# Unpacking the first MLP's wide weights through two tiles instead of one

## The chip, the cores and the metric

One NeuronCore of a Trainium2 chip runs the whole program. The metric is device time in microseconds (us) from the start to the end of one execution; smaller is better.

## The reference

```python
def reference(...):                               # float64 inputs, float32 result
    attn = g * mem_out + (1 - g) * softmax(causal(q @ k.T / 8)) @ v    # 4 x 8 heads, 576 x 64
    x = attn.transpose(0, 2, 1, 3).reshape(2304, 512)
    h = x @ w_in                                  # moe_w_in 512 x 2048, first MLP
    g = where(h > 0, h, exp(min(h, 0)) - 1)       # ELU
    x = g @ w_out                                 # moe_w_out 2048 x 512
    h = x @ w2_in                                 # second MLP, same sizes
    return maximum(0.01 * h, h) @ w2_out          # leaky ReLU
```

`mem_out` is a linear-attention read of a stored memory. The weights arrive as 64-bit floats. [...]

## The kernel before

**Blocks.** The 2048 hidden units of an MLP are 16 blocks of 128, called block 0 to 15 here (`f` in the code, `NF` = 16). A block's input and output weights go together into one weight place, a tile `w0`, `w1`, ... of 128 x 2 x 2 x 512: the rounded part ("hi") and the remainder ("lo") of 2 x 512 weights, so that three matmuls (hi x hi, lo x hi, hi x lo) give nearly full precision. The pool `wpa` has 7 places for blocks 0 to 6 (`NFA` = 7), the pool `wpb` 9 places for blocks 7 to 15. The second MLP's blocks use the same places later.

**Stages.** While attention still runs, TensorE already computes blocks 0 to 6 of the first MLP for "narrow" parts of 288 tokens, eight in all. Their partial products are copied out of PSUM to tiles `st` by ScalarE and stored to DRAM (`ys0` to `ys7`). After attention the last narrow parts end, and blocks 7 to 15 follow in five "wide" passes over 512 tokens (the last has 256). The second MLP then runs in wide passes with all 16 blocks.

**One block of work.** `h_mm` gives the hidden units (12 matmuls into one of four PSUM banks, two tagged `pm` and two `tp`). `elu` does a Relu and an Exp on ScalarE and a combining step on VectorE, which is the last reader of the bank; `g_split` casts the result to `gh` on VectorE and subtracts to get `gl` on GpSimd. The output product takes 12 matmuls more from `gh` and `gl` (`o_mm`).

**Unpacking** (`load_w`). For each block two transfers of 512 KB bring raw words into `wraw` (two buffers). Then: a ScalarE copy of the high words (L127) into a tile `wm`, three VectorE steps on 1024 int32 per partition (L128, L129, L132), a ScalarE cast to the hi part (L241), and two GpSimd subtractions to the lo part (L138). `wm` has one buffer in this stage (`nwm` = 1), so the next block's L127 waits for this block's second L138.

**Order.** A scheduler fixes, when the program is built, the order of instructions on every engine from priorities and its own estimates; each engine then executes its list in that order and waits on semaphores. The two `merge`d lists are the remaining narrow work (`side`) and the unpacking of blocks 7 to 12 (`NPRE` = 6); blocks 13 to 15 are unpacked within the first wide pass.

Of the kernel before, what the change touches and what calls it, by code (L numbers as in the profile page):

```python
# [9 lines left out]
F32R = mybir.dt.float32r  # L10
I32 = mybir.dt.int32
AF = mybir.ActivationFunctionType
ALU = mybir.AluOpType
AX = mybir.AxisListType

P = 128
# [3 lines left out]
def _f(ap):  # L20
    return ap.bitcast(F32)
# [3 lines left out]
def kernel(  # L25
# [14 lines left out]
    nc = tc.nc  # L40
    B, H, S, D = q.shape
    NT, DM = out.shape
# [3 lines left out]
    NF = DFF // P  # L46
    NFA = 7
    NPRE = 6
# [8 lines left out]
    E_GH, E_WH, E_VH, E_MS, E_V32, E_XH, E_RS, E_Y = "V", "A", "V", "P", "P", "A", "P", "A"  # L57
# [16 lines left out]
    wpa = ctx.enter_context(tc.tile_pool(name="wpa", bufs=1, side="left"))  # L74
# [18 lines left out]
    def load_w(key, pool, src_i, src_o, f, slot):  # L93

        w = pool.tile([P, 2, 2, DM], F32R, tag=f"w{slot}", name=f"w{slot}")
        wi_tiles[key, f] = w[:, :, 0].rearrange("p t (c n) -> p t c n", c=NKC)  # L100
        wo_tiles[key, f] = w[:, :, 1]
        raw = pools["wst"].tile([P, 2, DM, 2], I32, tag="wraw", bufs=2, name="wraw")
        nc.sync.dma_start(
            raw[:, 0].rearrange("p (c n) t -> p c (n t)", c=NKC),
            src_i[:, f * 2 * P:(f + 1) * 2 * P].rearrange("(c p) n -> p c n", p=P),
        )
        nc.sync.dma_start(raw[:, 1].rearrange("p n t -> p (n t)"), src_o[f * P:(f + 1) * P, :])
        if pools["decode_bank"]:
            for a in range(2):
                lw, hw = raw[:, a, :, 0], raw[:, a, :, 1]  # L110
                t = bank(pools["decode_bank"])
                m = t.bitcast(I32)
                nc.scalar.activation(out=t, in_=_f(hw), func=AF.Copy, scale=2.0 ** -112)
                nc.vector.tensor_scalar(out=m, in0=m, scalar1=3, scalar2=None, op0=ALU.logical_shift_left)
                nc.vector.scalar_tensor_tensor(
                    out=m, in0=lw, scalar=29, in1=m, op0=ALU.logical_shift_right, op1=ALU.bitwise_or
                )
                nc.vector.scalar_tensor_tensor(
                    out=m, in0=hw, scalar=-(1 << 31), in1=m, op0=ALU.bitwise_and, op1=ALU.bitwise_or
                )  # L120
                copy(E_WH, w[:, 0, a], t)
                nc.vector.tensor_tensor(out=w[:, 1, a], in0=t, in1=_f(w)[:, 0, a], op=ALU.subtract)
            return
        rw = raw.rearrange("p a n t -> p (a n) t")
        lw, hw = rw[:, :, 0], rw[:, :, 1]
        m = pools["wst"].tile([P, 2 * DM], I32, tag="wm", bufs=pools["nwm"], name="wm")
        nc.scalar.activation(out=_f(m), in_=_f(hw), func=AF.Copy, scale=2.0 ** -112)  # L127
        nc.vector.tensor_scalar(out=m, in0=m, scalar1=3, scalar2=None, op0=ALU.logical_shift_left)  # L128
        nc.vector.scalar_tensor_tensor(  # L129
            out=m, in0=lw, scalar=29, in1=m, op0=ALU.logical_shift_right, op1=ALU.bitwise_or  # L130
        )
        nc.vector.scalar_tensor_tensor(  # L132
            out=m, in0=hw, scalar=-(1 << 31), in1=m, op0=ALU.bitwise_and, op1=ALU.bitwise_or
        )
        t = _f(m).rearrange("p (a n) -> p a n", a=2)
        copy(E_WH, w[:, 0], t)
        for a in range(2):
            nc.gpsimd.tensor_tensor(out=w[:, 1, a], in0=t[:, a], in1=_f(w)[:, 0, a], op=ALU.subtract)  # L138
# [10 lines left out]
    def halves(n):  # L149
# [18 lines left out]
        out=mask[:, 448:576], in_=mask[:, 448:576], pattern=[[-1, 128]], compare_op=ALU.is_ge,  # L168
# [3 lines left out]
    pools = {"wst": wst_a.__enter__(), "nwm": 2, "decode_bank": "po"}  # L172
# [33 lines left out]
    def bank(tag):  # L206
        return psum.tile([P, 512], F32, tag=tag, bufs=BANKS[tag], name=tag)
# [30 lines left out]

    def copy(eng, dst, src):
        if eng == "A":  # L240
            nc.scalar.copy(dst, src)  # L241
        else:
            (nc.vector if eng == "V" else nc.gpsimd).tensor_copy(dst, src)  # L243

    def split(hi, lo, src, full=False):
        if full:
# [354 lines left out]
    def mtile(tag, bufs, dt=F32, shape=None):  # L601
        shape = shape or (NW,)
        pool = pools.get(("own", tag), pools["mlp"])
        return pool.tile([P] + list(shape), dt, tag=tag, bufs=bufs, name=tag)
# [12 lines left out]
    def h_mm(ph, wi, xh, xl):  # L617
        n_mm = 0
        for kc in range(NKC):
            for wj, xx in ((0, xh), (1, xh), (0, xl)):  # L620
                nc.tensor.matmul(ph, wi[:, wj, kc, :], xx[:, kc, :], start=n_mm == 0, stop=n_mm == 11)  # L621
                n_mm += 1

    def g_split(g, w):
        gh = mtile("gh", NG, F32R)[:, 0:w]
        gl = mtile("gl", NG, F32R)[:, 0:w]
        copy("A" if attending else E_GH, gh, g)
        nc.gpsimd.tensor_tensor(out=gl, in0=g, in1=_f(gh), op=ALU.subtract)  # L628
        return gh, gl

    def elu(ph, w):
        e = mtile("e", EB)[:, 0:w]
        nc.scalar.activation(out=e, in_=ph, func=AF.Relu, scale=-1.0)
        nc.scalar.activation(out=e, in_=e, func=AF.Exp, scale=-1.0)
        nc.vector.scalar_tensor_tensor(out=e, in0=e, scalar=-1.0, in1=ph, op0=ALU.add, op1=ALU.max)  # L635
        return g_split(e, w)

    def leaky(ph, w):
        t = mtile("e", EB)[:, 0:w]
# [4 lines left out]
    def o_mm(py, fs, key, ec, gs, first, last, opens=True, closes=True):  # L644
        for f in fs:
            wo = wo_tiles[key, f]
            gh, gl = gs[f]
            for n_mm, (wj, gg) in enumerate(((0, gh), (1, gh), (0, gl))):
                nc.tensor.matmul(  # L649
                    py, wo[:, wj, ec * P:(ec + 1) * P], gg,  # L650
                    start=opens and f == first and n_mm == 0, stop=closes and f == last and n_mm == 2,
                )

    attending = True
# [3 lines left out]
    def h_bank():  # L658
        nonlocal n_ph
        n_ph += 1  # L660
        return bank("tp" if tail and n_ph % 2 else "pm")
# [132 lines left out]
    attending = False  # L794
    edge = ctx.enter_context(tc.tile_pool(name="edge2", bufs=1, side="right"))
    edge.tile([P, 120], F32, name="edge2")
    wpb = ctx.enter_context(tc.tile_pool(name="wpb", bufs=1, side="right"))
# [3 lines left out]
    pools["xs"] = ctx.enter_context(tc.tile_pool(name="xs", bufs=1, side="right"))  # L801


    wun = [(1, lambda f=f: load_w(0, wpb, w1i, w1o, f, f - NFA)) for f in range(NFA, NF)]
    tail = True
    while ("cast", 1) not in pools:
# [8 lines left out]
    wun = wun[NPRE:]  # L815
# [32 lines left out]
    def load2(t0, n):  # L848
        xs = wide_x()
        for x, scr in zip(xs, xp_scr):  # L850
            recut(_f(x), scr, t0, n)
        return [x[:, :, 0:n] for x in xs]
# [6 lines left out]
    for gi, (t0, w) in enumerate(wide):  # L859
        gs = {}  # L860
        pys = {}

        def emit_out(f):
            for ec in range(NKC):
                if f == NFA:
                    pys[ec] = bank(("sc", "sc", "sc", "po")[ec])[:, 0:w]
                o_mm(pys[ec], [f], 0, ec, gs, NFA, NF - 1)
            del gs[f]

        ys = []  # L870

        def fetch_y():
            ne = NKC * TN // w
            for e in range(NKC // ne):
                yt = mtile("yx"[e], 1, F32, (ne, w))
                for pi, (_, _, pw, tok) in enumerate(parts):
                    lo, hi = max(tok, t0), min(tok + pw, t0 + w)
                    if lo < hi:
                        nc.sync.dma_start(
                            yt[:, :, lo - t0:hi - t0], y_scr[pi][:, ne * e:ne * e + ne, lo - tok:hi - tok]  # L880
                        )
                ys.extend(yt[:, i] for i in range(ne))

        for f in range(NFA, NF):
            if wun:
                wun.pop(0)[1]()
            if f == NFA + 3:
                fetch_y()
            ph = h_bank()[:, 0:w]
            h_mm(ph, wi_tiles[0, f], *cur)  # L890
            gs[f] = elu(ph, w)
            if f > NFA + 1:
                emit_out(f - 2)
            if gi >= 1 and f - NFA in (W2A, W2B) and len(w2) > NF - NFA:
                w2.pop(0)()
        emit_out(NF - 2)
        if gi + 1 < len(wide):
            cur = load2(*wide[gi + 1])
        emit_out(NF - 1)
        for ec in range(NKC):  # L900
            x1 = ys[ec]
            nc.vector.tensor_tensor(out=x1, in0=pys[ec], in1=x1, op=ALU.add)
            nc.sync.dma_start(x1_scr[gi][:, ec], x1)
# [81 lines left out]
```

## Time and profile before

| | us |
|---|---|
| median of 3 runs | 1069.39 (1069.12 to 1070.02) |
| the profiled execution | 1069.05 |
| span of its instructions | 1067.2 |
| TensorE busy | 1040.3 (97% of the span) |
| VectorE, ScalarE, GpSimd busy | 591.8, 485.2, 531.6 |
| granted TensorE clock | 0.996 of full speed |

The span is what the profile shows; the 1.85 us beside it lie before the first and after the last instruction. Attention ends at about 390 us, the last narrow part at about 452 us, the first wide pass lies from 441 to about 513 us.

### The profile page before, as it was taken

What the parts mean: (1) busy time and instruction counts of PE and PEld (TensorE: products, weight loads), DVE (VectorE), ACT (ScalarE), POOL (GpSimd) and SP (SyncE); (2) the same over time, 40 slices, a digit from 0 to 9 for tenths busy, and PEclk for the clock granted to TensorE, in tenths of its full rate; (3) what the DMA queues carried; (4) which work ended last, traced back from release to release, by engine and by line L of the source; (5) the groups of instructions that cost most, each with busy time, mean ns of one, the idle gap of its engine ahead of it and who ended that gap; (6) DMA issues with size and microseconds to landing.
All of it is one profiled execution on the core that took longest, in us unless ns stands there. A gap on an engine that the chain in (4) does not pass through costs nothing.

```text
span 1067.2 us, 17324 instructions
## 1 busy us (share of the span) xinstructions
PE 1040.3 (97%) x5904; PEld 909.9 (85%) x5904; DVE 591.8 (55%) x1380; ACT 485.2 (45%) x1171; POOL 531.6 (50%) x674
## 2 busy tenths in 40 slices
PE   7998899999999999999999999999999999999998
PEld 4786799989998999977888889888888888888897
DVE  6889987888888746566773324654322221232232
ACT  5999887787878735444442225332211211111111
POOL 7675775677668634464643225855422422322222
PEclk9999999999999999999999999999999999999999
DMA  7754553564456249465672304430200100000010
GB/s 183 195 150 112 160 142 96 139 166 142 115 128 164 90 113 337 147 223 168 227 232 85 119 1 138 158 119 1 80 1 1 60 20 1 8 33 1 1 40 20
DMA packets 150120, 115.05 MB, mean 108 GB/s; under 512 B 80016, under 2 KB 141456, under 8 KB 150032
## 3 DMA queue, kind: packets, MB, share of 16 engines
q1 hardware_dynamic: 149888, 113.68, 36.2%
q8 instruction: 47, 0.77, 0.3%
q14 instruction: 41, 0.34, 0.1%
q10 hardware_dynamic: 144, 0.26, 0.1%
HBM read 78.52 MB, written 31.85 MB: 103 GB/s over the span
## 4 chain that ended last, share of the span: by engine, by line
PE 80%; DVE 7%; DMA 4%; ACT 3%; issue 2%; POOL 2%; SPq 1%; DVEq 0%; POOLq 0%; ACTq 0%
PE pm L621 18%; PE sc L919 14%; PE tp L621 14%; PE sc L649 7%; PE pm L649 5%; PE po L919 4%; PE tp L457 4%; PE po L524 4%; PE pm L524 2%; PE po L649 2%; PE sc L426 2%; PE sc L428 1%; PE sc L429 1%; POOL w L138 1%; DMA wraw<-in_moe_w_in_dram 1%
## 5 line engine op out<-in xcount | busy, mean ns | idle before, releaser
L628 POOL TENSOR_TENSOR gl<-e,gh 128x512 fp32r<-128x512 f32 (+2 forms) x181 | 200.4, 1111 | 371.9 <-DVE gh L243 267.8
L621 PE MATMUL tp<-xw,w 128*128 128x512 f32 (+1 forms) x504 | 144.6, 367 | 1.7 <-DVE e L635 1.7
L621 PE MATMUL pm<-xw,w 128*128 128x512 f32 (+1 forms) x496 | 142.7, 369 | 1.2 <-ACT w L241 1.2
L919 PE MATMUL sc<-w,gh 128*128 128x512 f32 x448 | 135.9, 390 | 0.0
L451 POOL TENSOR_SCALAR pt<-pt,rs,omg 128x128 f32<-128x128 f32 (+4 forms) x160 | 104.1, 660 | 21.2 <-DVE rs L446 17.2
L621 PEld LDWEIGHTS tp<-xw,w 128*128 128x128 f32 x504 | 91.8, 188 | 18.3 <-DVE e L635 2.2
L621 PEld LDWEIGHTS pm<-xw,w 128*128 128x128 f32 x496 | 90.5, 188 | 17.7 <-ACT w L241 1.6
L436 ACT ACTIVATE pt<-pt,mx 128x128 f32<-128x128 f32 (+4 forms) x160 | 93.3, 585 | 23.2 <-DVE mx L431 21.6
L649 PE MATMUL sc<-gh,w 128*128 128x512 f32 (+2 forms) x438 | 103.2, 340 | 0.2 <-DVE gh L243 0.2
L919 PEld LDWEIGHTS sc<-w,gh 128*128 128x128 f32 x448 | 83.2, 188 | 16.5
L621 PE MATMUL tp<-xv,w 128*128 128x512 f32 (+1 forms) x252 | 92.6, 367 | 0.0
L621 PE MATMUL pm<-xv,w 128*128 128x512 f32 (+1 forms) x248 | 91.4, 369 | 0.0
L640 ACT ACTIVATE e<-pm 128x512 f32<-128x512 f32 (+1 forms) x40 | 22.2, 555 | 144.7 <-PE pm L621 141.7
L138 POOL TENSOR_TENSOR w<-wm,w 128x512 fp32r<-128x512 f32 x50 | 65.8, 1337 | 43.4 <-ACT w L241 39.4
L457 PE MATMUL tp<-ident,pt 128*128 128x128 f32 x480 | 82.0, 276 | 3.0 <-DVE al L250 1.5
L641 DVE TENSOR_TENSOR e<-tp,e 128x512 f32<-128x512 f32 (+1 forms) x40 | 25.5, 637 | 106.8 <-ACT e L640 106.8
L919 PE MATMUL sc<-w,gl 128*128 128x512 f32 x224 | 84.3, 389 | 0.0
L649 PEld LDWEIGHTS sc<-gh,w 128*128 128x128 f32 x438 | 74.6, 188 | 9.1 <-DVE gh L243 0.6
L641 DVE TENSOR_TENSOR e<-pm,e 128x512 f32<-128x512 f32 (+1 forms) x40 | 25.5, 637 | 102.1 <-ACT e L640 102.1
L621 PE MATMUL pm<-xh,w 128*128 128x288 f32 x368 | 79.6, 302 | 1.7 <-ACT xh L610 1.6
L243 DVE CAST gh<-e 128x512 fp32r<-128x512 f32 (+2 forms) x146 | 71.0, 490 | 13.5 <-PE po L919 3.0
L640 ACT ACTIVATE e<-tp 128x512 f32<-128x512 f32 (+1 forms) x40 | 22.2, 554 | 117.4 <-PE tp L621 117.4
(162 smaller groups left out, 2447.5 us busy)
## 6 DMA issues: line engine op xcount, KB each, us to landing
wraw<-in_moe_w_in_dram SPq DMA_DIRECT2D x32, 512.0 KB, 3.9
wraw<-in_moe_w_out_dram SPq DMA_DIRECT2D x32, 512.0 KB, 4.8
xh<-xh SPq DMA_DIRECT2D x8, 576.0 KB, 3.3
xl<-xl SPq DMA_DIRECT2D x8, 576.0 KB, 4.0
ys<-st SPq DMA_DIRECT2D x32, 144.0 KB, 2.8
x<-x1s SPq DMA_DIRECT2D x9, 512.0 KB, 3.8
vn<-in_v_dram SPq DMA_DIRECT2D x64, 64.0 KB, 2.4
out_dram<-st SPq DMA_DIRECT2D x32, 128.0 KB, 1.7
```

The source lines that it names most:

```text
L138: nc.gpsimd.tensor_tensor(out=w[:, 1, a], in0=t[:, a], in1=_f(w)[:, 0, a], op=ALU.subtract)
L243: (nc.vector if eng == "V" else nc.gpsimd).tensor_copy(dst, src)
L436: nc.scalar.activation(out=pt[0:m, 0:nk], in_=pt[0:m, 0:nk], func=AF.Exp, scale=-1.0, bias=mx[0:m, last:last + 1], accum_out=self.pd["ss"] ...
L451: nc.gpsimd.tensor_scalar(out=pt, in0=pt, scalar1=rs[0:m, i:i + 1], scalar2=omg[0:m, h:h + 1], op0=ALU.mult, op1=ALU.mult,)
L457: nc.tensor.transpose(dst, self.p[c][:, k0:k0 + kn], ident)
L524: nc.tensor.matmul(po[:, a:b], w, x, start=i == 0, stop=i == len(mms) - 1)
L621: nc.tensor.matmul(ph, wi[:, wj, kc, :], xx[:, kc, :], start=n_mm == 0, stop=n_mm == 11)
L628: nc.gpsimd.tensor_tensor(out=gl, in0=g, in1=_f(gh), op=ALU.subtract)
L640: nc.scalar.mul(t, ph, 0.01)
L641: nc.vector.tensor_tensor(out=t, in0=ph, in1=t, op=ALU.max)
L649: nc.tensor.matmul(py, wo[:, wj, ec * P:(ec + 1) * P], gg, start=opens and f == first and n_mm == 0, stop=closes and f == last and n_mm == 2,)
L919: nc.tensor.matmul(pos[tb], gg[:, tb * P:(tb + 1) * P], wo[:, wj, :], start=f == 0 and n_mm == 0, stop=f == NF - 1 and n_mm == 2,)
```

## The change

Every second unpacked block uses, in place of `wm`, the first half of a weight place that nobody needs at that time: blocks 8, 10 and 12 use `w6` of `wpb` (the place of block 13, not yet filled), block 14 uses `w0` of `wpa` (block 0 of the first MLP, which is finished by then). So two blocks can be in work at once. In the first wide pass the unpacking of blocks 13, 14 and 15 is put behind the ELU of blocks 8, 9 and 11 on each engine.

```diff
@@ load_w
-        m = pools["wst"].tile([P, 2 * DM], I32, tag="wm", bufs=pools["nwm"], name="wm")
+        if f in pools.get("spare", ()):
+            home, place = pools["spare"][f]
+            t = home.tile([P, 2, 2, DM], F32R, tag=f"w{place}", name=f"w{place}")
+            m = t.rearrange("p a b n -> p (a b n)")[:, 0:2 * DM].bitcast(I32)
+        else:
+            m = pools["wst"].tile([P, 2 * DM], I32, tag="wm", bufs=pools["nwm"], name="wm")
@@ g_split, elu: remember the cast, the subtraction and the Exp
+        pools["elu"] = [hi.ins, lo.ins]
+        pools["elu"].append(ex.ins)
@@ before the last narrow work
+    pools["spare"] = {f: (wpb, NPRE) for f in range(NFA + 1, NFA + NPRE, 2)}
+    pools["spare"].update({f: (wpa, 0) for f in range(NFA + NPRE + 1, NF, 2)})
@@ first wide pass
+        if gi == 1:
+            pools["spare"].clear()
         for f in range(NFA, NF):
-            if wun:
-                wun.pop(0)[1]()
             ...
             gs[f] = elu(ph, w)
+            if wun and f - NFA in (1, 2, 4):
+                with ExitStack() as order:
+                    for ins in pools["elu"]:
+                        order.enter_context(tc.issue_after(ins))
+                    wun.pop(0)[1]()
```

**First place: ScalarE, end of the last narrow part.** In these rows `st<-sc` is the copy of the last narrow part's products out of PSUM, `e<-tp` and `e<-pm` of 512 are the first wide Relus (blocks 7 and 8), and `w_7155` and `w_7167` are the weight places of blocks 11 and 12. Before:

```order
L127 ACTIVATE wm<-wraw 128x1024
L241 CAST w_7093<-wm 128x1024
L241 COPY st<-sc 128x288 x2
L127 ACTIVATE wm<-wraw 128x1024
L241 COPY st<-sc 128x288 x2
L241 CAST w_7155<-wm 128x1024
L633 ACTIVATE e<-tp 128x512
L633 ACTIVATE e<-pm 128x512
L634 ACTIVATE e<-e 128x512 x2
```

Now (the lines are L132 for L127, L246 for L241, L638 and L639 for L633 and L634; `w_7171` is the borrowed place of block 12):

```order
L132 ACTIVATE wm<-wraw 128x1024
L638 ACTIVATE e<-pm 128x288
L639 ACTIVATE e<-e 128x288
L132 ACTIVATE w_7171<-wraw 128x1024
L246 CAST w_7155<-wm 128x1024
L246 CAST w_7167<-w_7171 128x1024
L246 COPY st<-sc 128x288 x4
L638 ACTIVATE e<-tp 128x512
L638 ACTIVATE e<-pm 128x512
L639 ACTIVATE e<-e 128x512 x2
```

The four copies and the wide Relus stood behind the unpacking of block 10 and beside that of block 11; now they stand behind the casts of blocks 11 and 12.

**Second place: VectorE, last narrow part.** `gh<-e` is the cast of an ELU's result, `e<-e,pm` its combining step. Before, around the unpacking of block 9:

```order
L128 TENSOR_SCALAR wm<-wm 128x1024
L129 SCALAR_TENSOR_TENSOR wm<-wraw,wm 128x1024
L635 SCALAR_TENSOR_TENSOR e<-e,pm 128x288
L635 SCALAR_TENSOR_TENSOR e<-e,tp 128x288
L132 SCALAR_TENSOR_TENSOR wm<-wraw,wm 128x1024
L243 CAST gh<-e 128x288 x2
L635 SCALAR_TENSOR_TENSOR e<-e,pm 128x288
L243 CAST gh<-e 128x288
L128 TENSOR_SCALAR wm<-wm 128x1024
```

Now, blocks 9 (`wm`) and 10 (the borrowed `w_7097`); L133, L134, L137 are the three steps and L247 is the cast:

```order
L133 TENSOR_SCALAR wm<-wm 128x1024
L134 SCALAR_TENSOR_TENSOR wm<-wraw,wm 128x1024
L247 CAST gh<-e 128x288 x3
L137 SCALAR_TENSOR_TENSOR wm<-wraw,wm 128x1024
L133 TENSOR_SCALAR w_7097<-w_7097 128x1024
L640 SCALAR_TENSOR_TENSOR e<-e,tp 128x288
L134 SCALAR_TENSOR_TENSOR w_7097<-wraw,w_7097 128x1024
L247 CAST gh<-e 128x288
L137 SCALAR_TENSOR_TENSOR w_7097<-wraw,w_7097 128x1024
L640 SCALAR_TENSOR_TENSOR e<-e,pm 128x288
```

Before, all seven casts of the last narrow part stood ahead of block 10's steps; now four of them stand among the steps of blocks 9 and 10, two between those of blocks 10 and 11, and the last behind the third step of block 11.

## Rows read from the trace of the kernel before

**Rows 1.** Waits of TensorE from 380 us on: total, times, longest.

```profile
PE tp L621 <- DVE e L635: 1.7, 1, 1.7
PE pm L621 <- ACT w L241: 1.2, 1, 1.2
PE sc L649 <- DVE gh L243: 0.2, 1, 0.2
```

**Rows 2.** Timeline of TensorE: start, us, [idle before <- releaser].

```profile
454.03 0.62 PE L621 MATMUL pm<-xw,w 128*128 128x512 f32 x2
454.49 0.39 PE L621 MATMUL pm<-xv,w 128*128 128x512 f32 x1
456.62 0.73 PE L621 MATMUL tp<-xw,w 128*128 128x512 f32 x2 [1.74 <-DVE e L635]
...
473.39 1.66 PE L649 MATMUL sc<-gh,w 128*128 128x512 f32 x6 [0.15 <-DVE gh L243]
...
483.03 0.97 PE L621 MATMUL pm<-xw,w 128*128 128x512 f32 x3 [1.19 <-ACT w L241]
```

**Rows 3.** Waits of ScalarE from 400 to 560 us.

```profile
ACT wm L127 <- POOL w L138: 34.7, 15, 3.5
```

**Rows 4.** Timeline of ScalarE, end of the last narrow part.

```profile
430.71 1.15 ACT L127 ACTIVATE wm<-wraw 128x1024 f32<-128x1024 f32 x1 [1.09 <-POOL w L138]
...
445.19 1.05 ACT L241 CAST w<-wm 128x1024 fp32r<-128x1024 f32 x1 [3.28 <-DVE wm L132]
446.15 0.69 ACT L241 COPY st<-sc 128x288 f32<-128x288 f32 x2
...
451.13 0.40 ACT L241 COPY st<-sc 128x288 f32<-128x288 f32 x1 [1.12 <-DMA ys<-st]
452.42 0.40 ACT L241 COPY st<-sc 128x288 f32<-128x288 f32 x1 [0.89 <-PE sc L649]
453.30 1.05 ACT L241 CAST w<-wm 128x1024 fp32r<-128x1024 f32 x1 [0.48 <-DVE wm L132]
454.25 0.59 ACT L633 ACTIVATE e<-tp 128x512 f32<-128x512 f32 x1
```

**Rows 5.** DMA issues from 446.5 to 447.3 us: KB, median us to landing.

```profile
ys<-st SPq DMA_DIRECT2D x2, 144.0 KB, 4.5
```

**Rows 6.** DMA issues from 417 to 419 us (raw words of block 9).

```profile
wraw<-in_moe_w_out_dram SPq DMA_DIRECT2D x1, 512.0 KB, 8.8
```

**Rows 7.** Waits of SyncE's DMA queue from 395 to 560 us.

```profile
SPq L103 <- DVE wm L132: 78.9, 14, 9.0
```

**Rows 8.** Timeline of SyncE's DMA queue, issue of block 9's raw words.

```profile
417.99 0.94 SPq L107 DMA_DIRECT2D wraw<-in_moe_w_out_dram  x1
```

**Rows 9.** Timeline of VectorE, steps alone and steps beside GpSimd.

```profile
422.37 0.69 DVE L128 TENSOR_SCALAR wm<-wm 128x1024 int32<-128x1024 int32 x1 [4.67 <-ACT wm L127]
423.10 1.23 DVE L129 SCALAR_TENSOR_TENSOR wm<-wraw,wm 128x1024 int32<-128x1024 int32 x1
...
424.61 1.22 DVE L132 SCALAR_TENSOR_TENSOR wm<-wraw,wm 128x1024 int32<-128x1024 int32 x1
...
426.11 0.52 DVE L243 CAST gh<-e 128x288 fp32r<-128x288 f32 x2
...
455.88 0.69 DVE L635 SCALAR_TENSOR_TENSOR e<-e,tp 128x512 f32<-128x512 f32 x1 [2.62 <-ACT e L634]
...
458.14 1.40 DVE L128 TENSOR_SCALAR wm<-wm 128x1024 int32<-128x1024 int32 x1 [0.30 <-ACT wm L127]
459.57 2.20 DVE L129 SCALAR_TENSOR_TENSOR wm<-wraw,wm 128x1024 int32<-128x1024 int32 x1
```

**Rows 10.** Timeline of GpSimd, subtractions alone and beside VectorE.

```profile
426.58 1.58 POOL L628 TENSOR_TENSOR gl<-e,gh 128x288 fp32r<-128x288 f32 x2 [5.40 <-DVE gh L243]
...
454.42 2.51 POOL L138 TENSOR_TENSOR w<-wm,w 128x512 fp32r<-128x512 f32 x2 [5.57 <-ACT w L241]
457.67 3.02 POOL L628 TENSOR_TENSOR gl<-e,gh 128x512 fp32r<-128x512 f32 x2 [0.74 <-DVE gh L243]
```

More of the change, by code (lines that the diff above doesn't have):

```diff
@@ L240, in copy @@
         if eng == "A":
-            nc.scalar.copy(dst, src)
-        else:
-            (nc.vector if eng == "V" else nc.gpsimd).tensor_copy(dst, src)
+            return nc.scalar.copy(dst, src)
+        return (nc.vector if eng == "V" else nc.gpsimd).tensor_copy(dst, src)
     def split(hi, lo, src, full=False):
@@ L626, in g_split @@
         gl = mtile("gl", NG, F32R)[:, 0:w]
-        copy("A" if attending else E_GH, gh, g)
-        nc.gpsimd.tensor_tensor(out=gl, in0=g, in1=_f(gh), op=ALU.subtract)
+        hi = copy("A" if attending else E_GH, gh, g)
+        lo = nc.gpsimd.tensor_tensor(out=gl, in0=g, in1=_f(gh), op=ALU.subtract)
+        pools["elu"] = [hi.ins, lo.ins]
         return gh, gl
@@ L633, in elu @@
         nc.scalar.activation(out=e, in_=ph, func=AF.Relu, scale=-1.0)
-        nc.scalar.activation(out=e, in_=e, func=AF.Exp, scale=-1.0)
+        ex = nc.scalar.activation(out=e, in_=e, func=AF.Exp, scale=-1.0)
         nc.vector.scalar_tensor_tensor(out=e, in0=e, scalar=-1.0, in1=ph, op0=ALU.add, op1=ALU.max)
-        return g_split(e, w)
+        g = g_split(e, w)
+        pools["elu"].append(ex.ins)
+        return g
     def leaky(ph, w):
```

## The prediction

> **What bounds the kernel now.** I read the waits of TensorE first. From 380 us on it waits three times, 3.08 us in all [rows 1, 2], and all three lie in the first wide pass, beside the unpacking. The change moves nothing ahead of the last narrow part, and the matmuls are the same, so it can win these waits back or add others.
>
> The timeline shows what a wait costs [rows 2]. Two 512-column matmuls follow each other in 0.46 us (454.03 to 454.49), so the matmul after 454.49 was due at 454.72. It starts at 456.62: 1.90 us late, where the row says 1.74 idle, and the first pair then takes 0.73 in place of 0.62. A stop costs about 0.27 us on top of its idle time. Three stops: 3.08 + 3 x 0.27 = 3.9 us. That is the most that can be won: 1069.05 - 3.9 = 1065.1, for the profiled execution's own time, which lies 0.3 under the median of 1069.39. About 0.2% (2.1 us) is what a measurement of this kernel can tell from no change.
>
> Who makes TensorE wait? The long stop waits for VectorE's combining step of block 7, which frees a `tp` bank. On ScalarE [rows 4] the Relu of block 7 starts at 454.25, since it is queued behind the four copies `st<-sc` (446.15 to 452.82) and a cast. The third copy waits for the first two's stores to land, 4.5 us [rows 5]. The 1.19 us stop waits for a cast of block 12, the end of the serial chain: 15 times, 34.7 us in all, ScalarE's L127 waits for GpSimd to free `wm` [rows 3].
>
> **What the change does, part by part.**
>
> *The wait for `wm`.* It goes for every second block. Block 9's L127 started at 430.71, after 1.09 us of idle time behind GpSimd [rows 4]. Its raw words, issued last at 417.99 [rows 8], landed 8.8 us later [rows 6], at 426.8; the issue waits for block 7's third VectorE step, as most of these issues do [rows 7], and that comes no sooner now. So block 9 enters VectorE at 426.8 + 1.15 = 428.0, against 431.9 before, and block 10 stands behind it at once: its words come right behind. The gain at the entrance is 4 us, and no longer the GpSimd wait but the transfer sets it.
>
> *The order.* The copies, and with them the Relu of block 7, now stand behind the casts of blocks 11 and 12, where they stood behind block 10's. Before TensorE gets its bank, VectorE must therefore finish four blocks' steps from 428.0 on. Before, it finished block 10 by 445.2 and the copies went off at 446.15. This is the step on which everything rests.
>
> *VectorE and GpSimd together.* Alone, the three steps take 0.69 + 1.23 + 1.22 = 3.14 us and a 288-wide cast 0.26 [rows 9]; a pair of lo subtractions takes 2.51, a `gl` 0.79 [rows 10]. Beside GpSimd the same steps take 1.40 and 2.20 [rows 9]. The two `gl` of 457.67 to 460.69 took 3.02 in place of about 2.6 [rows 10], the first step ran from 458.14 to 459.54, and the second, issued at 459.57, ended at 461.77: 1.08 after GpSimd's end at 460.69. So the two engines take turns: each waits out the other's instruction and then runs 0.15 us shorter than alone. The combining step reads PSUM and is not held: it started at 455.88 and took 0.69 [rows 9] while GpSimd subtracted from 454.42 to 456.93 [rows 10].
>
> The work that takes turns between 428.0 and the end of block 12's third step is: 4 x 3.14 = 12.6 of steps, 7 casts = 1.8, 7 `gl` = 5.5, and the lo subtractions of blocks 9, 10 and the first of block 11, 2.5 + 2.5 + 1.3 = 6.3. Sum 26.2; with some 15 changes of turn at 0.15 less, 23.9. That ends at 428.0 + 23.9 = 451.9; going through the queues instruction by instruction with these durations I get 451.4, and take it. Bounds: if the turns never collided, VectorE alone needs 12.6 + 1.8, four combining steps at 0.4 (0.69 for 512 columns [rows 9], scaled to 288), and a pause of 2.2 for ScalarE between blocks 10 and 11 (a cast 1.05 and a copy 1.15 [rows 4]): 18.2, so 446.2. With no shortening at the turns: 454.2. Between them I take the middle, since the collisions stand in the rows.
>
> The Trainium skill ("SBUF — State Buffer", section "SBUF: two separate sides") says that VectorE and GpSimd hold a shared port for a whole instruction and that the other blocks fully. By that alone the sum would be 26.2 and the last step at 454.2; by the rows, which show the blocked instruction 0.15 us shorter, it is 23.9.
>
> *From there to TensorE.* Cast of block 12: 1.05, so the first copy at 452.4. The store of the first copy goes behind the raw words of block 14, as it went behind block 11's before, and lands 4.5 us after its issue at 452.8 [rows 5]: 457.3. Two copies (0.7) and the way from the Relu's start to TensorE's restart, 456.62 - 454.25 = 2.37 [rows 2, 4]: 460.4. Due at 454.72, TensorE is 5.7 us late, where it was 1.9. The waits that TensorE meets before that, on `gh` and `gl` of the last narrow part, are part of these 5.7, not added to them; I expect them between 433 and 448, some 3 to 4 us in pieces under 1 us each.
>
> *Later.* The unpacking of blocks 13 to 15 behind the ELUs takes the cast of block 12 and the short third stop away (1.19 and 0.15 idle, 2.0 with restarts). In their place the `gl` of block 11 stands on GpSimd behind the two lo subtractions of block 14, among which block 15's steps take their turns. From the restart TensorE has 86 matmuls at 0.23 before it wants this `gl`, to about 480; by the same durations the `gl` comes between 480 and 481.5. I add 0.7, with 0 and 2 as bounds. From the second wide pass on the unpacking goes as before, one tile, and TensorE waited for nothing there [rows 1]; nothing is added.
>
> *The sum.* 1069.05 - 3.9 (all old stops) + 5.7 (the bank of block 7) + 0.3 (restarts of the small stops) + 0.7 (later) = 1071.8; as against the median, +2.4 us. I say 1071.7.
>
> **The rivals.**
>
> *A, faster: the collisions miss each other.* VectorE ends block 12 near 446, the first copy is at 447, the store lands near 452, and TensorE restarts at 454.7, when it is due. All old stops go: 1065.1 to 1066.5. Best Practices of the Trainium skill ("Trainium Kernel Development and Optimization") asks for double buffers; it would have this outcome, since the 34.7 us of waits for one tile disappear. For it: the scheduler put the order so. Against it: the steps of 1.40 and 2.20 in the rows. The point from which it decides is the first copy `st<-sc` of the last part: before 447, faster.
>
> *B, one wait for another.* The turns cost half of what I sum: block 12 ends near 449, TensorE restarts near 458, 3.3 late, and nothing new comes later. 1069.05 - 3.9 + 3.3 + 0.3 = 1068.7, with the later 0 to 2 us 1068.7 to 1070.7.
>
> *C, slower still.* Full turns (454.2) and the full later wait: 8.1 + 2 - 3.9 + 0.5: 1075.7. Speaking for it: with 8.8 us to landing there [rows 6], block 10's words may come later than right behind block 9's, and all else by as much.
>
> **How the numbers follow.** My forecast, slower by 1.5 to 4 us, has 0.45, C 0.07; B 0.30; A 0.18. Over 0.2% slower is all above 1071.5: about 0.50, which is C and most of the forecast. Within 0.2% (1067.3 to 1071.5): 0.32. Faster: 0.18. The predicted time is that of the forecast. The range 1067.0 to 1074.8 leaves out most of A and the outer part of C; the forecast's own range is 1070.5 to 1073.5.
>
> **What would show it.** Right: TensorE's wait for VectorE's combining step L640 (L635 before) grows or moves to after 458, with small waits on `gh` and `gl` (L247, L632) between 432 and 448; ScalarE's first copy of the last part at 451 to 453; no wait of TensorE for a cast of weights; among blocks 9 to 12 most second steps take over 1.8 us. Wrong: that copy before 447, or steps at 1.23; or a wait of TensorE after 500 us, of which I allow for none.

## The result and the profile after

The changed kernel takes 1074.30 us (median of 6 runs, 1073.49 to 1078.09), the kernel before 1069.26 us in the runs beside it. The ratio is 1.0051, 95% interval 1.0036 to 1.0066: slower by half a per cent, or 5.0 us. The forecast was 1071.7, slower by 2.4 us, with 1067.0 to 1074.8 as its range. The sign and the order of the steps held. The size did not: the loss is twice the forecast's, and the time lies above the forecast's own narrower range (1070.5 to 1073.5) and only 0.5 us under the end of the wide one. Four executions of 1156 to 5513 us (two of the kernel before, one each of runs 2 and 4 below) are left out of the ratios here.

The profiled execution of the changed kernel took 1078.09 us and was the slowest of the six. Some 4.45 us of that lie ahead of the change, in attention, whose instructions are the same in both kernels. There TensorE was granted 1.2 GHz for 17.1 us in all, against 6.8 us in the profiled execution of before. One such stretch, by windows (the last three figures are the granted clock, the DMA share and GB/s):

```profile
327.90:331.20 3.30, 3.30 (x16) 3.24 (x16) 3.21 (x10) 2.41 (x7) 3.30 (x5) 0.50 0.74 244
```

In the same window of before the clock was 1.00. So times of after are read here less 4.45 us where they are set beside times of before. From the 2,801st matmul (of 5,904) to the last, which leaves attention out, TensorE takes 645.5 us before and 650.1 after: the change costs 4.6 us in these two executions, and this is the figure that is explained below. Matmuls are compared with their twins by their place in the order; in the last narrow part the two orders differ, and by the 2,998th matmul both kernels have done the same work again.

TensorE's waits after, from 385 us on, answer to [rows 1]:

```profile
PE sc L656 <- POOL gl L632: 2.0, 4, 1.0
PE tp L625 <- DVE e L640: 1.6, 1, 1.6
PE sc L656 <- DVE gh L247: 0.8, 1, 0.8
```

The wait for a weight cast (L246, 1.2 us before) is gone. The wait for the combining step L640 is still there, and waits for `gh` and `gl` have joined it. Where they lie, TensorE's timeline shows, against [rows 2]:

```profile
441.08 0.80 PE L656 MATMUL sc<-gh,w 128*128 128x288 f32 x4 [0.78 <-DVE gh L247]
...
462.67 0.39 PE L625 MATMUL pm<-xv,w 128*128 128x512 f32 x1
464.63 0.73 PE L625 MATMUL tp<-xw,w 128*128 128x512 f32 x2 [1.57 <-DVE e L640]
...
485.54 0.50 PE L656 MATMUL sc<-gl,w 128*128 128x512 f32 x1 [0.98 <-POOL gl L632]
```

There are three places. Small stops lie between 438 and 452, in the last narrow part. One of 1.96 us from start to start (462.67 to 464.63) stands at the bank of block 7, and late ones from 484 us on. By how late each matmul starts against its twin of before, less the 4.45, TensorE is 3.7 us behind at the end of the small stops and 4.6 at the end of the program. Idle time alone (4.4 us against 3.1 in [rows 1]) would have told too little: of the small stops' 3.7 us less than half is idle time (0.24, 0.78 and 0.47), and the rest lies in drawn-out starts, 0.24 to 0.50 us behind the matmul ahead in place of 0.13 to 0.23.

What ScalarE does ahead of the bank, against [rows 4]:

```profile
431.22 1.14 ACT L132 ACTIVATE wm<-wraw 128x1024 f32<-128x1024 f32 x1 [1.54 <-DMA wraw<-in_moe_w_out_dram]
433.76 1.17 ACT L132 ACTIVATE w<-wraw 128x1024 f32<-128x1024 f32 x1 [1.40 <-DMA wraw<-in_moe_w_out_dram]
...
455.78 1.06 ACT L246 CAST w<-w 128x1024 fp32r<-128x1024 f32 x1 [3.74 <-DVE w L137]
456.74 0.68 ACT L246 COPY st<-sc 128x288 f32<-128x288 f32 x2
461.56 0.79 ACT L246 COPY st<-sc 128x288 f32<-128x288 f32 x2 [4.14 <-DMA ys<-st]
462.25 0.60 ACT L638 ACTIVATE e<-tp 128x512 f32<-128x512 f32 x1
```

Blocks 9 and 10 follow each other by 2.5 us, and both now wait for their raw words, not for GpSimd. The cast of block 12 waits 3.74 us for VectorE, the copies stand behind it, and the Relu of block 7 behind the copies.

VectorE and GpSimd in blocks 11 and 12, against [rows 9, 10]:

```profile
447.00 2.20 DVE L134 SCALAR_TENSOR_TENSOR wm<-wraw,wm 128x1024 int32<-128x1024 int32 x1
...
449.49 1.46 DVE L137 SCALAR_TENSOR_TENSOR wm<-wraw,wm 128x1024 int32<-128x1024 int32 x1
...
451.81 1.70 DVE L134 SCALAR_TENSOR_TENSOR w<-wraw,w 128x1024 int32<-128x1024 int32 x1
453.55 2.20 DVE L137 SCALAR_TENSOR_TENSOR w<-wraw,w 128x1024 int32<-128x1024 int32 x1
```

```profile
448.08 1.79 POOL L632 TENSOR_TENSOR gl<-e,gh 128x288 fp32r<-128x288 f32 x1
...
452.39 4.51 POOL L143 TENSOR_TENSOR w<-wm,w 128x512 fp32r<-128x512 f32 x2
```

Steps that take 1.22 us alone take 1.46 to 2.20 here; a `gl` of 0.79 alone takes 1.79, and a pair of lo subtractions 4.51 in place of 2.51.

### The profile page after: what moved, and what is told of

Same layout as the page of the kernel before. It is cut to its first block, busy times and chain, and to the rows that moved or that the text cites. A ratio compares the mean times of both kernels' runs of the same rounds, so it can differ in the third digit from the quotient of the medians.

```text
span 1076.3 us, 17322 instructions
## 1 busy us (share of the span) xinstructions
PE 1046.2 (97%) x5904; PEld 913.2 (85%) x5904; DVE 596.8 (55%) x1380; ACT 484.1 (45%) x1171; POOL 539.2 (50%) x674
## 4 chain that ended last, share of the span: by engine, by line
PE 81%; DVE 8%; DMA 4%; issue 3%; ACT 2%; SPq 1%; POOL 1%; DVEq 0%; ACTq 0%; POOLq 0%
PE pm L625 19%; PE sc L933 14%; PE tp L625 14%; PE sc L656 7%; PE pm L656 5%; PE po L933 4%; PE tp L461 4%; PE po L528 4%; PE pm L528 2%; PE po L656 2%; PE sc L432 2%; PE sc L433 2%; PE sc L430 1%; DMA wraw<-in_moe_w_in_dram 1%; DVE pt L435 1%
## 5 line engine op out<-in xcount | busy, mean ns | idle before, releaser
L632 POOL TENSOR_TENSOR gl<-e,gh 128x512 fp32r<-128x512 f32 (+2 forms) x181 | 203.0, 1124 | 398.1 <-DVE gh L247 283.8
L247 DVE CAST gh<-e 128x512 fp32r<-128x512 f32 (+2 forms) x146 | 70.8, 488 | 13.4 <-PE po L933 2.8
L435 DVE CUSTOM_DVE_ANT_0 pt<-sc,mask 128x128 f32<-128x128 f32 (+4 forms) x160 | 69.3, 444 | 9.8 <-PE sc L433 4.6
```

What stands on the lines that cost most here:

```text
L247: return (nc.vector if eng == "V" else nc.gpsimd).tensor_copy(dst, src)
L435: nc.vector.tensor_tensor_reduce(out=pt[0:m, k0:k0 + n], in0=sc[0:m, 0:n], in1=mk, op0=ALU.add, op1=ALU.min, scale=-0.125, scalar=mx[0:m, ...
L632: lo = nc.gpsimd.tensor_tensor(out=gl, in0=g, in1=_f(gh), op=ALU.subtract)
```

## The experiments

Each run was timed in several rounds beside the kernel before, which measured 1069.29, 1069.76 and 1069.56 in the three groups (runs 1 to 4, 5 to 8, 9 and 10). "Stretch" is the time from the 2,801st matmul's start to the last's in the profiled execution, which leaves attention out. It is one execution for each run, so a difference of some tenths in it shows nothing.

| run | median us | ratio to before (95%) | stretch us |
|---|---|---|---|
| before | 1069.26 | 1 | 645.5 |
| after | 1074.30 | 1.0051 (1.0036 to 1.0066) | 650.1 |
| 1 placing alone | 1069.97 | 1.0005 (0.9996 to 1.0014) | 645.3 |
| 2 two tiles alone | 1082.89 | 1.0126 (1.0111 to 1.0142) | 657.9 |
| 3 after, four places | 1073.09 | 1.0037 (1.0025 to 1.0050) | 648.8 |
| 4 before, four places | 1071.58 | 1.0022 (1.0013 to 1.0032) | 647.6 |
| 5 after, one tile late | 1071.91 | 1.0023 (1.0012 to 1.0035) | 647.5 |
| 6 after, lo on VectorE | 1068.97 | 0.9995 (0.9986 to 1.0003) | 644.0 |
| 7 before, lo on VectorE | 1067.25 | 0.9978 (0.9968 to 0.9987) | 643.2 |
| 8 second tile for block 8 only | 1071.13 | 1.0013 (1.0004 to 1.0021) | 646.9 |
| 9 runs 5 and 6 together | 1068.20 | 0.9988 (0.9979 to 0.9997) | 644.3 |
| 10 runs 4 and 7 together | 1068.44 | 0.9989 (0.9980 to 0.9997) | 644.2 |

The theory was that of the prediction (T): two blocks in work at once make VectorE and GpSimd take turns, and put the copies and the Relu of block 7 behind the casts of blocks 11 and 12. The rival (P): the placing of blocks 13 to 15 behind the ELUs is what costs.

**Run 1: the placing alone.** One tile for all blocks.

```diff
-    pools["spare"] = {f: (wpb, NPRE) for f in range(NFA + 1, NFA + NPRE, 2)}
-    pools["spare"].update({f: (wpa, 0) for f in range(NFA + NPRE + 1, NF, 2)})
+    pools["spare"] = {}
```

> The changed kernel with one unpacking tile for all blocks; only the placing of blocks 13 to 15 behind the wide ELUs is left of the change. Theory T (two blocks in work at once put the last narrow part's copies, and with them TensorE's bank for block 7, behind the casts of blocks 11 and 12): ScalarE's order up to block 12 is that of the kernel before, so TensorE stops at block 7 for 1.5 to 2 us as before, and the time is within 1.2 us of before: 1068.5 to 1070.5. Rival P (the placing behind the ELUs is what costs): most of the 5 us stays, 1072 to 1074.5.

Measured 1069.97. TensorE has the three waits of before, at the same places:

```profile
PE tp L625 <- DVE e L640: 1.5, 1, 1.5
PE pm L625 <- ACT w L246: 1.2, 1, 1.2
PE sc L656 <- DVE gh L247: 0.2, 1, 0.2
```

The placing costs nothing that can be measured. P falls, and all the rest hangs on the second tile.

**Run 2: the two tiles alone.** Blocks 13 to 15 unpacked ahead of blocks 7 to 9 of the wide pass, as in the kernel before.

```diff
         for f in range(NFA, NF):
+            if wun:
+                wun.pop(0)[1]()
...
-            if wun and f - NFA in (1, 2, 4):
-                with ExitStack() as order:
...
-                    wun.pop(0)[1]()
```

> The changed kernel with blocks 13 to 15 unpacked where the kernel before unpacks them, ahead of blocks 7 to 9 of the wide pass; only the turns of tiles are left of the change. Theory T: ScalarE now also meets the first step of block 13 ahead of the copies, and the cast of block 13 and the first steps of blocks 14 and 15 between the copies and the Relu of block 7, so TensorE's long stop grows by 4 to 5 us against the changed kernel, while the later waits for gl of blocks 11 and 12 (about 2.5 us) go: 1075 to 1079. Rival P: the time falls back to 1069 to 1071.

Measured 1082.89, in T's direction and beyond its figure. The rows of ScalarE and of TensorE, and the windows while TensorE stood and after it restarted:

```profile
458.51 1.05 ACT L246 CAST w<-wm 128x1024 fp32r<-128x1024 f32 x1 [0.74 <-DVE wm L137]
459.46 1.12 ACT L132 ACTIVATE w<-wraw 128x1024 f32<-128x1024 f32 x1
460.49 0.38 ACT L246 COPY st<-sc 128x288 f32<-128x288 f32 x1
463.48 1.14 ACT L132 ACTIVATE wm<-wraw 128x1024 f32<-128x1024 f32 x1 [2.61 <-DMA wraw<-in_moe_w_out_dram]
464.53 0.57 ACT L638 ACTIVATE e<-tp 128x512 f32<-128x512 f32 x1
```

```profile
469.64 1.22 PE L625 MATMUL tp<-xw,w 128*128 128x512 f32 x2 [10.17 <-DVE e L640]
```

```profile
459.90:463.40 3.50, 0.00 (x0) 0.00 (x0) 2.75 (x2) 0.97 (x2) 2.67 (x2) 1.00 0.99 354
...
463.60:473.90 10.30, 4.26 (x10) 3.40 (x11) 8.23 (x9) 5.02 (x7) 7.28 (x5) 0.50 1.05 344
```

The Relu of block 7 stands behind work of three more blocks, and one of the steps ahead of it waits 2.61 us for block 15's raw words, a wait that the expectation did not have. VectorE adds to it: its combining step stands behind block 15's third step (466.81, 2.17 us long), so the way from the Relu's start to TensorE's restart is 5.1 us in place of 2.4.

```profile
468.91 0.68 DVE L640 SCALAR_TENSOR_TENSOR e<-e,tp 128x512 f32<-128x512 f32 x1
```

The stop grows from 1.96 to 10.57 us (459.07 to 469.64). TensorE's clock stands at 0.50 (1.2 GHz) in the window from 463.6, within the stop, to 473.9, and its first 10 matmuls after the restart go at 0.43 us in place of 0.23, some 2 us more. So the placing behind the ELUs is what keeps the second tile from costing 13.6 us.

**Run 3: four places for the copies.** The last narrow part's four results go to four places, so no copy waits for a store.

```diff
-                y = mtile("st", 2)[:, 0:w]
+                if closing and pi == mine[1][0]:
+                    if ec == 0:
+                        st["y4"] = rows("x", pi, w)
+                    y = st["y4"][:, ec]
+                else:
+                    y = mtile("st", 2)[:, 0:w]
```

> The changed kernel, but the four copies of the last narrow part go to four places in the home of block 15, which is not in use then, in place of two buffers by turns; the order on ScalarE is unchanged. Theory T: the wait of the third copy for a store to land (4.14 us in the changed kernel's profile) goes, the Relu of block 7 starts that much sooner and TensorE's long stop, some 5.7 us late in all with the small waits before it, shrinks by 3.5 to 4.1: 1070 to 1071, or up to 1072 if the later waits for gl grow. Rival P, and a rival by which TensorE would have been late there anyway (the small waits on gh and gl alone): 1073.5 to 1074.5.

Measured 1073.09, the stretch 1.3 us shorter than after's: neither figure of T (3.5 to 4.1) nor nothing. ScalarE shows why (the new places are part of a weight place, so the copies are listed as `w<-sc`):

```profile
453.39 0.99 ACT L246 COPY w<-sc 128x288 f32<-128x288 f32 x3
457.25 0.40 ACT L246 COPY w<-sc 128x288 f32<-128x288 f32 x1 [2.87 <-PE sc L656]
457.54 0.60 ACT L638 ACTIVATE e<-tp 128x512 f32<-128x512 f32 x1
```

Three copies go at once, but the fourth waits for TensorE itself, which the small stops have made 3.7 us late by then. TensorE's stop at the bank shrinks from 1.96 to 0.56 us. So of the lateness at block 7, some 5.5 us, the small stops make 3.7 whatever the copies do; the store adds the rest. The expectation took the 4.14 us wait of one engine for time that the end would get back.

**Run 4: the same four places in the kernel before.**

> The kernel before with the same four places for the last narrow part's copies. Theory T: its long stop of 1.9 us at block 7 goes, the short ones for the cast of block 12 and gh may stay or grow: 1066.5 to 1068. A rival by which a stop that goes comes back later (the casts of blocks 12 and 13 are late anyway): 1068.5 to 1069.5.

A miss: 1071.58, slower. The fourth copy waits for TensorE (2.36 us) in this kernel too, and the scheduler now puts the cast of block 11 between the Relu and the Exp of block 7, where it stood ahead of the Relu in [rows 4]. The unpacking behind comes later, and TensorE waits for it, and once for a `gh`, from then on:

```profile
476.48 0.50 PE L621 MATMUL tp<-xw,w 128*128 128x512 f32 x1 [0.43 <-POOL w L138]
483.67 0.50 PE L649 MATMUL sc<-gh,w 128*128 128x512 f32 x1 [1.68 <-DVE gh L243]
493.74 0.50 PE L621 MATMUL tp<-xw,w 128*128 128x512 f32 x1 [1.62 <-ACT w L241]
```

**Run 5: one tile for blocks 13 to 15.** After run 3 the question was where the late waits come from.

```diff
-    pools["spare"].update({f: (wpa, 0) for f in range(NFA + NPRE + 1, NF, 2)})
```

> The changed kernel, but blocks 13 to 15 take turns on the one tile wm only (block 14 no longer in the place w0); two tiles up to block 12 as in the change. Theory T2 (after the first four runs: 3.7 us are lost by small waits for gh and gl of the last narrow part among the steps of blocks 9 to 12, 2 us at the bank of block 7, and 2.5 to 3 us later, where the gl of blocks 11 and 12 stands behind the lo subtractions of two blocks in work at once): the small waits and the bank stay, the later waits for gl (1.37, 0.69, 0.5) go: 1071.2 to 1072.5. Rival: the later waits belong to the placing behind the ELUs, which stays: 1073.8 to 1075. The placing with one tile throughout measured 1069.97 without them, which speaks for T2.

Measured 1071.91, the stretch 2.6 us shorter than after's. The small stops and the bank (2.11 us from start to start) are as in after; behind the bank TensorE has no stop left, and the waits for `gl` and `gh` in these rows are the small stops:

```profile
PE tp L625 <- DVE e L640: 1.7, 1, 1.7
PE sc L656 <- POOL gl L632: 1.0, 2, 0.5
PE sc L656 <- DVE gh L247: 0.8, 1, 0.8
```

The late 2.6 us belong to the second tile (place `w0`) of block 14, not to the placing.

**Run 6: the lo subtractions on VectorE.** This tells turns between the engines from a queue that is merely full.

```diff
-            nc.gpsimd.tensor_tensor(out=w[:, 1, a], in0=t[:, a], in1=_f(w)[:, 0, a], op=ALU.subtract)
+            (nc.gpsimd if key else nc.vector).tensor_tensor(out=w[:, 1, a], in0=t[:, a], in1=_f(w)[:, 0, a], op=ALU.subtract)
```

> The changed kernel, but the two lo subtractions of a first-MLP block run on VectorE in place of GpSimd. Theory T2 with the turns: a pair costs GpSimd 2.51 us alone and up to 4.6 beside VectorE's steps; on VectorE it is about 1.2 (half of a third step's 1.22 each), GpSimd is free for gl, and the steps run near their durations alone. Small waits for gl go from 433 to 452 and the later ones too: 1070 to 1073. Rival Q (no turns decide it, VectorE's queue is simply full with two blocks in work): VectorE gets 1.2 us more per block, gh comes later still, the bank of block 7 as well: 1075 to 1078.

Measured 1068.97, better than T2's 1070 to 1073, and far from Q's 1075 to 1078: VectorE has more to do and is done sooner. Its groups for blocks 9 to 12, first after (432 to 456 us), then this run (428 to 452 us); the mean of one in ns stands ahead of the last bar:

```profile
L137 DVE SCALAR_TENSOR_TENSOR w<-wraw,w 128x1024 int32<-128x1024 int32 x2 | 4.5, 2250 | 0.0
L134 DVE SCALAR_TENSOR_TENSOR wm<-wraw,wm 128x1024 int32<-128x1024 int32 x2 | 3.4, 1714 | 0.1
L137 DVE SCALAR_TENSOR_TENSOR wm<-wraw,wm 128x1024 int32<-128x1024 int32 x2 | 3.3, 1648 | 0.0
L134 DVE SCALAR_TENSOR_TENSOR w<-wraw,w 128x1024 int32<-128x1024 int32 x2 | 3.2, 1580 | 0.0
```

```profile
L143 DVE TENSOR_TENSOR w<-w,w 128x512 fp32r<-128x512 f32 x4 | 3.2, 837 | 1.1 <-ACT w L246 1.1
L143 DVE TENSOR_TENSOR w<-wm,w 128x512 fp32r<-128x512 f32 x4 | 2.6, 684 | 0.0
L134 DVE SCALAR_TENSOR_TENSOR w<-wraw,w 128x1024 int32<-128x1024 int32 x2 | 2.5, 1225 | 0.1
L134 DVE SCALAR_TENSOR_TENSOR wm<-wraw,wm 128x1024 int32<-128x1024 int32 x2 | 2.4, 1221 | 0.0
L137 DVE SCALAR_TENSOR_TENSOR wm<-wraw,wm 128x1024 int32<-128x1024 int32 x2 | 2.4, 1221 | 0.0
L137 DVE SCALAR_TENSOR_TENSOR w<-wraw,w 128x1024 int32<-128x1024 int32 x2 | 2.4, 1219 | 0.0
```

The eight second and third steps take 14.4 us in after and 9.7 here, each at its 1.22 us alone. The 5.8 us of subtractions that VectorE takes on are mostly paid by that, and GpSimd is rid of four pairs, 10 us even at their 2.51 alone. TensorE has only 0.9 us of idle waits left, and none at the bank of block 7. Rival Q falls. The run takes the lo subtractions out of the turns and out of GpSimd's queue ahead of `gl` at one stroke; how much of the gain is the one and how much the other, it does not separate. The order on ScalarE is not after's either: two of the four copies (445.53) go ahead of block 12's cast (449.23) here, so the gain at the bank of block 7 may in part be this. The small stops lie ahead of it, and they shrink from 3.7 to 1.0 us of lateness.

**Run 7: the same in the kernel before**, on its line L138.

> The kernel before with the same lo subtractions on VectorE. T2: the chain of one block gets shorter by about 1.3 us, block 12's cast comes earlier, its stop goes, and there are fewer turns: 1066 to 1069. Rival Q: VectorE's queue delays gh and the bank of block 7: 1070.5 to 1073.

Measured 1067.25, the fastest kernel here, 0.22% under before (ratio 0.9968 to 0.9987). Of TensorE's waits one is left, against three in [rows 1]:

```profile
PE tp L621 <- DVE e L635: 0.8, 1, 0.8
```

**Run 8: the second tile for block 8 only**, with one tile from block 9 on.

```diff
-    pools["spare"] = {f: (wpb, NPRE) for f in range(NFA + 1, NFA + NPRE, 2)}
-    pools["spare"].update({f: (wpa, 0) for f in range(NFA + NPRE + 1, NF, 2)})
+    pools["spare"] = {f: (wpb, NPRE) for f in (NFA + 1,)}
```

> The changed kernel with a second tile for block 8 alone; blocks 9 to 15 take turns on wm. T2: while TensorE works on the last narrow part, one block is in work at a time, the small waits for gh and gl shrink to under 1 us in all, and there are no later waits for gl: 1068 to 1070. A rival by which the placing of the copies alone decides (ScalarE has one of the four copies behind the cast of block 11 here): 1071 to 1073.

Half a hit. The small stops are gone, as T2 said, but the time is the rival's, 1071.13. The scheduler puts the fourth copy behind the cast of block 11, and the Relu of block 7 behind the first step of block 12 as well; TensorE stops for 3.07 us at the bank, and its clock falls behind that stop, which costs some 1.6 us more in this execution (whether it fell in the others is not shown):

```profile
458.58 0.73 PE L625 MATMUL tp<-xw,w 128*128 128x512 f32 x2 [2.68 <-DVE e L640]
```

```profile
459.90:463.40 3.50, 3.50 (x10) 2.73 (x9) 1.04 (x3) 2.31 (x4) 2.63 (x3) 0.51 1.13 352
```

So the order on ScalarE can make TensorE late without the small stops, and the small stops without the wait for a store (run 3).

**Runs 9 and 10: the edits that helped, together.** Run 9 is run 6 with run 5's edit, run 10 is run 7 with run 4's.

> The changed kernel with the lo subtractions of the first MLP on VectorE and one tile for blocks 13 to 15 (the two edits that each took time away, together). If they add: the run with lo on VectorE (1068.97) still waited later for gl and gh of blocks 11 and 12, about 1.5 us with restarts, and these go: 1067 to 1068.2. Rival: with one tile the chain of blocks 12 to 15 gets longer and a cast of weights comes late again, as in the kernel before: 1068.5 to 1070.

> The kernel before with the lo subtractions on VectorE (1067.25) and four places for the last narrow part's copies. It stopped once more, 1.22 us at the bank of block 7 (its Relu stands behind the fourth copy, which waits for a store and for the cast of block 11). If the store is what it waits for: 1065.5 to 1066.5. Rival: the fourth copy comes behind the cast and the first step of block 12 on ScalarE anyway (451.90 to 453.02, then the copy at 452.92), so nothing is won: 1067 to 1067.5.

Neither adds up. Run 9 (1068.20, at the edge of its first range) loses the late stops, and gains a new one in the second wide pass:

```profile
539.06 0.50 PE L656 MATMUL sc<-gh,w 128*128 128x512 f32 x1 [1.00 <-DVE gh L247]
```

In run 10 (1068.44) the stop at the bank stays at 1.25 us (1.22 in run 7), as its rival said, since the fourth copy stands behind the cast of block 11 and the first step of block 12 there, store or no store. It is over a microsecond slower than run 7 (the intervals overlap; the stretches differ by 1.1 us), which the rival did not have; short stops at a `gh` and a `gl`, at 495.4 and 539.2 us, are new.

## Why the prediction was right, step by step

The table sets its steps beside the profile after, less 4.45 us.

| step | predicted | measured |
|---|---|---|
| block 9's first step on VectorE | 428.0 | 432.39 - 4.45 = 427.9 |
| block 12's third step ends | 451.4 (446.2 to 454.2) | 455.75 - 4.45 = 451.3 |
| first copy of the last part | 452.4 | 456.74 - 4.45 = 452.3 |
| third copy, behind the store's landing | 457.3 | 461.56 - 4.45 = 457.1 |
| TensorE restarts at block 7 | 460.4, 5.7 late | 464.63 - 4.45 = 460.2, 5.5 late |
| small waits ahead of it | 433 to 448, 3 to 4 us | 433.7 to 447.3, 3.7 us |
| later waits | +0.7 (0 to 2) | about +3.0 (what remains of the 4.6) |

**The entrance and the turns held.** Block 9 waits for its transfer, at the time worked out from the landing [rows 6]. From there to the end of block 12's third step it took 23.4 us; the sum with turns, shortened by 0.15 us at each change, was 23.9, and going through the queues gave 23.4. By the rule of the Trainium skill ("SBUF — State Buffer", section "SBUF: two separate sides") that one engine blocks the other for a whole instruction, the sum was 26.2; the rows agree with the rule's sense and not with its full figure. Rival A (the collisions miss each other) fell at the place named for it: the copy came at 452.3, not before 447. The Trainium skill (Best Practices, "Trainium Kernel Development and Optimization") asks for double buffers so that DMA and compute overlap. The second tile here lets engines overlap: between 400 and 510 us ScalarE's waits for GpSimd to free a tile fell from 21.1 us to 8.0. The time went up all the same: run 1 without the second tile is 4.3 us faster than after with it.

One sign was put too strongly: "most second steps over 1.8 us" is true of one in four (1.23, 1.46, 2.20, 1.70). With the third steps, seven of eight take longer than alone, and run 6 shows what they take without GpSimd's lo subtractions. In the sum of rival C the step to 454.2 is 2.8 us past 451.4, so its 8.1 should be 8.5.

**The bank of block 7 was sized rightly; its cause was given in part.** "The order" was called the step on which everything rests. The time came out, but runs 3 and 8 show two things that each make TensorE late at this bank, and the later one counts: the small stops (3.7 us by themselves) and the copies ahead of the Relu. The prediction counted the small waits as part of the 5.7, which is right as a sum, but they are not a by-product of the copies' order: they stay when the copies' wait goes.

**The term that was mis-sized is the later one: +0.7 taken, 2 as its bound, about 3.0 measured** (4.6 in all, less 5.5, and the 3.9 of old stops that went). The wait that it named came when it said. The `gl` of block 11 was to come between 480 and 481.5. GpSimd's rows show it behind block 14's lo subtractions, to 485.48, which is 481.0 on the clock of before:

```profile
480.10 3.18 POOL L143 TENSOR_TENSOR w<-w,w 128x512 fp32r<-128x512 f32 x2
483.24 2.24 POOL L632 TENSOR_TENSOR gl<-e,gh 128x512 fp32r<-128x512 f32 x1
487.73 2.54 POOL L143 TENSOR_TENSOR w<-wm,w 128x512 fp32r<-128x512 f32 x2 [2.25 <-DVE gh L247]
490.23 1.29 POOL L632 TENSOR_TENSOR gl<-e,gh 128x512 fp32r<-128x512 f32 x1
```

What the working left out is what follows: the next `gl`, of block 12, stands in the same way behind block 15's pair (487.73), with a stop of 0.69 us from start to start, then a `gh` (0.51), each with a drawn-out start of 0.34 us behind it. A `gh` near 549 us costs some 0.3, a small wait after 500 us, of which none was allowed for. Run 5 takes 2.6 us of this away by putting block 14 back on the one tile. With this term at its measured size the sum is 1069.05 - 3.9 + 5.5 + 3.0 = 1073.7. That is the profiled execution of after less its 4.45 us, as it must be, since the 3.0 is a remainder; the median of after is 1074.30. The range held because it was wide; the term's own bound of 2 did not.

**The old stops went** as counted: no wait for a cast of weights is left, so the change did win its 3.9 us, and gave back 8.5. The reason given was wrong in two points, which the number did not show. The stop of 1.19 us was not for block 12, whose cast starts at 463.06, but for block 14, whose cast ends where TensorE goes on (483.03 in [rows 2]):

```profile
481.94 1.04 ACT L241 CAST w<-wm 128x1024 fp32r<-128x1024 f32 x1 [3.28 <-DVE wm L132]
```

And it was not the placing that took it away. Run 1 has the placing and still has the stop; with the second tile the cast of block 14 starts at 477.26, which is 472.8 on the clock of before, 9 us sooner. That the count came out all the same was luck in this part.

## What to carry to other kernels

Before adding a second buffer, ask whether the engines behind it can work on both fills at once. Here the wait for one tile had kept VectorE's steps and GpSimd's subtractions apart, and taking it away made both engines slower and put other work later. Where two engines take turns, try moving work from one of them to the other before adding buffers: the subtractions on VectorE gained 2.5 us in the kernel before, and in the changed one took back its whole loss. A long wait on one engine is not the time to be won; look at what would be last without it (run 3: 4.1 us of wait, 1.3 us of gain), and when one stop of a series is found, cost the next instance of it too.

## What the runs showed of the hardware that was not expected

TensorE's clock fell to 1.2 GHz within the stop of 10.57 us (run 2) and behind the one of 3.07 us (run 8, clock 0.51 from 459.9 to 463.4), while after's 1.96 us and run 5's 2.11 us stops were not followed by a fall. In run 8 the fall came 1.4 us after the restart, when TensorE was already busy, and seven matmuls took 0.43 us and two 0.33 in place of 0.23: some 1.6 us on top of the 3.07.

A pair of lo subtractions takes 2.51 us on GpSimd alone, up to 4.51 beside VectorE's steps, and 1.29 on VectorE (446.77 to 448.06 in run 6).
